# Ninety-two more products behind the last transposes of a fused convolution and two feed-forward layers

## The chip, the cores and the metric

The kernel runs on one core of a Trainium2 chip. The metric is the device time of one execution in microseconds. The kernel before took 1194.71 and 1194.87 us in two runs, with a median of 1194.79.

## The reference

Two batches of 4096 tokens with 192 numbers each go through a short causal convolution (7 taps, weights by softmax, one set for each of 8 groups of 24 columns) and then through two feed-forward layers with 2048 hidden columns. Everything is fp32.

```python
w = np.exp(weight - weight.max(-1)); w = w / (w.sum(-1) + 1e-09)
out = np.einsum('hk,bskhg->bshg', w, x_unf)      # 7 taps along the sequence
h = x @ w_in;  g = np.maximum(0.01 * h, h);  x = g @ w_out
h = x @ w_in;  g = np.where(h >= 1, h, np.where(h <= -1, 0.0, (h + 1) ** 2 / 4));  out = g @ w_out
```

## The kernel before, in words

The 8192 tokens are cut into 16 blocks of T = 512. A block is held transposed: the 192 columns lie on partitions, 128 of them and 64 of them (DB), and the 512 tokens along the line. An fp32 value is split into a high and a low part of type fp32r, so that one exact product becomes several products of fp32r: x has the parts 0 and 1 for the first 128 columns and 2 and 3 for the other 64, stored twice on 128 partitions; the weights are wi_h, wi_l, wi_b and wo_h, wo_l, wo_b, each a resident tile of 16 chunks of 128 columns (NF = 16, 2048 numbers in a line).

The unit of work is one block, one layer and one chunk of 128 hidden columns. Its `up` (L584) does five products into a bank of PSUM, the other engines apply the activation and split the result into gh and gl, and its `down` (L593) does five products into two accumulator banks. There are 2 x 16 x 16 = 512 units, ten products each, 5120 in all; every product loads its own stationary tile of 128 x 128 and streams 512 columns.

Every step is given to a planner with an engine, a cost and a due time; it simulates the engines, and the steps are then issued in the order of their planned starts (`plan.order()`, the loop at the end of the kernel). Each engine works through its own list in this order.

At the start there are products of zeros in bf16 (L328), transposes of the input for the first three blocks (L478; 128 columns, or 64 for the second part), and some taps of the convolution as products in plain fp32 with a diagonal matrix (L529, with `rhs=t()[:, 1, 2 * k:2 * k + T]`, and L534); each product of plain fp32 stands as two records in the trace. In the first and the second layer together the units' banks are 0 to 3, the accumulators of the first layer 4 and 5, of the second 6 and 7.

The last block ends in `finish_last`. ACT copies one accumulator (L691), DVE the other (L692); the tensor engine turns them back with four products by an identity (L697, into bank 1) and four transposes (L706, into bank 0); DVE and ACT copy these into two output tiles (L714, L723), and each of the two tiles goes to memory with one transfer (L732), one issued by SP's queue and one by ACT's. The four transposes are the last entries of the tensor engine's list. At the end of the program SP's queue waits for the transfers, and then all engines meet (L803, the launch).

Of the kernel before, what the change touches and what calls it, by code (L numbers as in the profile page):

```python
# [145 lines left out]
def kernel(  # L146
# [16 lines left out]
    nc = tc.nc  # L163
# [6 lines left out]
    T = 512  # L170
# [34 lines left out]
    banks = [pp.tile([128, T], F32, name=f"bank{i}") for i in range(8)]  # L205
# [22 lines left out]
    wi_h = [cp.tile([128, NF, 128], F32R, name=f"wi_h{m}") for m in range(2)]  # L228
    wi_l = [cp.tile([128, NF, 128], F32R, name=f"wi_l{m}") for m in range(2)]
    wi_b = [cp.tile([128, NF, 128], F32R, name=f"wi_b{m}") for m in range(2)]  # L230
    wo_h = [cp.tile([128, NF, 128], F32R, name=f"wo_h{m}") for m in range(2)]
# [89 lines left out]
    def add_warm():  # L321
        nc.gpsimd.memset(zero, 0.0)
        out_ = bank(1, -10)
        for i in range(WARM):
            cold = i < COLD
            plan.add(
                pe, 430 if cold else 220,
                lambda: nc.tensor.matmul(  # L328
                    out=out_(), lhsT=zero, rhs=zero.unsqueeze(1).broadcast_to((128, T // 128, 128)),
                    start=True, stop=True,  # L330
                ),
                writes=[out_], due=-1e9 if cold else 1e9,
            )
# [53 lines left out]
    def add_diagonals():  # L387
        def fold():
            for e in range(2):
                nc.gpsimd.tensor_copy(same[DB * e:DB * (e + 1)], ident[DB * e:DB * (e + 1), DB * e:DB * (e + 1)])  # L390

        plan.add(pool, 500, lambda: make_identity(nc, ident), writes=["ident"])
        plan.add(pool, 260, fold, reads=["ident"], writes=["same"])
        for k in range(KP, K):
            plan.add(
                dve, 220,
                lambda k=k: nc.vector.tensor_scalar(flat(NP + k - KP), ident, taps[:, 0, k:k + 1], None, ALU.mult),
                reads=["ident", "taps"], writes=[("diagonal a", k)], uses=[spare],
            )
        for k in range(NP):  # L400
            plan.add(
                dve, 220,
                lambda k=k: nc.vector.tensor_scalar(
                    flat(k).rearrange("p (e d) -> p e d", e=2), same.unsqueeze(1).broadcast_to((128, 2, DB)),
                    pair[:, k:k + 1], None, ALU.mult,
                ),
                reads=["same", "pair"], writes=[("diagonal", k)], uses=[spare],
            )
# [327 lines left out]
            )  # L736


    units = []
    for i in range(NF + OFF[-1]):  # L740
        for j in range(N0):
# [2 lines left out]
    one = [(0, j, f) for j in range(N0, NB) for f in range(NF)]  # L744
    two = [(1, j, f) for j in range(NB) for f in range(NF)]
    while two:
        units += one[:1] + two[:1]
        one, two = one[1:], two[1:]
# [12 lines left out]
    with tc.manual_schedule():  # L761
        add_warm()
        add_taps()
        add_diagonals()
        seen = set()
        for t, (m, j, f) in enumerate(units):
            if m == 0 and f == 0:
                add_conv(t - AHEAD, j)
            for o in range(2):
                if (m, o, f // 2) not in seen:  # L770
                    seen.add((m, o, f // 2))
                    add_weights(t, m, o, f // 2)
            add_unit(t, (m, j, f))
        for tag, count in COUNT.items():
            plan.rotate(tag, count)
        for n in plan.order():
            plan.steps[n]["fn"]()


# [28 lines left out]
```

## Time and profile before

| what | before |
|---|---|
| median of two runs | 1194.79 us (1194.71 and 1194.87) |
| profiled execution, first to last instruction (span) | 1192.7 us |
| around the span | not recorded for the profiled execution; the two runs are 2.0 and 2.2 us longer than its span |
| tensor engine busy | 1186.8 us, 5210 products |
| weight loads | 972.7 us, 5210 |
| VectorE (DVE), ScalarE (ACT), GpSimd (POOL) busy | 782.7, 734.3, 438.2 us |
| mean granted clock of the tensor engine | 0.999 of 2.4 GHz |

PE stands for the tensor engine's products, PEld for its weight loads, which run beside the products. The records of consecutive products overlap, since a product takes longer from its start to its end than the next one has to wait; so the cost of a product in a stream is the distance from start to start. An instruction's line in the trace is the line of the kernel shown above. "x8" after a row means that eight instructions stand in it, and the time is from the first start to the last end.

### The profile page before, as it was taken

The numbers are of one execution on the slowest core, as the hardware profiler recorded it, in microseconds if no ns is written. First come the engines' busy times: TensorE is split into PE (matmuls) and PEld (weight loads), VectorE is DVE, ScalarE is ACT, GpSimd is POOL, SyncE is SP. The second block draws the span as 40 slices with busy tenths as digits, with TensorE's granted clock in tenths as the row PEclk, the third lists the DMA queues.
The fourth block names the chain that finished last, engine by engine and source line by source line (L and its number), as shares of the span: only waits on it lengthen the run. The fifth ranks groups of instructions, "written<-read, shape, count | busy, mean of one in ns | idle before, by whom it ended". The sixth has DMA issues, their size and how long they took to land.

```text
span 1192.7 us, 15464 instructions
## 1 busy us (share of the span) xinstructions
PE 1186.8 (100%) x5210; PEld 972.7 (82%) x5210; DVE 782.7 (66%) x1209; ACT 734.3 (62%) x1296; POOL 438.2 (37%) x407
## 2 busy tenths in 40 slices
PE   9999999999999999999999999999999999999998
PEld 5788888888888888888888888888888888888887
DVE  7899897748567494764847658485674545447664
ACT  6777866656565565655656566565655656556654
POOL 4566374323223232232323233232233222335554
PEclk9999999999999999999999999999999999999999
DMA  4443111101001010010101001010000000000000
GB/s 132 117 104 99 43 43 18 23 1 23 10 9 23 1 23 9 15 18 1 32 1 23 10 10 23 1 23 1 1 14 1 14 1 3 12 1 14 14 14 14
DMA packets 114000, 27.90 MB, mean 23 GB/s; under 512 B 103680, under 2 KB 111872, under 8 KB 113920
## 3 DMA queue, kind: packets, MB, share of 16 engines
q1 hardware_dynamic: 113504, 26.69, 10.3%
q8 instruction: 40, 0.66, 0.2%
q14 instruction: 40, 0.33, 0.1%
q10 hardware_dynamic: 416, 0.23, 0.1%
HBM read 20.61 MB, written 6.29 MB: 23 GB/s over the span
## 4 chain that ended last, share of the span: by engine, by line
PE 99%; DMA 0%; SPq 0%; DVE 0%; issue 0%; ACT 0%; ACTq 0%
PE bank L584 49%; PE bank L593 49%; PE bank L529 1%; DMA wraw<-in_x_dram 0%; PE bank L534 0%; PE bank L328 0%; PE bank L478 0%; SPq L257 0%; PE bank L697 0%; SPq L255 0%; DVE s L714 0%; SPq L469 0%; DVE s L723 0%; ACT s L723 0%; ACTq L723 0%
## 5 line engine op out<-in xcount | busy, mean ns | idle before, releaser
L632 POOL TENSOR_TENSOR gl<-g,gh 128x512 fp32r<-128x512 f32 x256 | 343.2, 1343 | 677.6 <-ACT gh L630 674.7
L619 DVE TENSOR_SCALAR s<-bank 128x512 f32<-128x512 f32 x256 | 176.3, 689 | 303.4 <-PE bank L584 302.2
L584 PE MATMUL bank<-x,wi_h 128*128 128x512 f32 x1024 | 317.5, 391 | 0.0
L584 PE MATMUL bank<-x,wi_b 128*128 128x512 f32 x1024 | 316.9, 391 | 0.0
L623 ACT ACTIVATE s<-s,half 128x512 f32<-128x512 f32 x256 | 184.8, 722 | 192.7 <-DVE s L619 191.4
L630 ACT CAST gh<-g 128x512 fp32r<-128x512 f32 x256 | 158.6, 620 | 180.8 <-DVE g L627 178.1
L584 PEld LDWEIGHTS bank<-x,wi_h 128*128 128x128 f32 x1024 | 191.9, 188 | 42.2 <-issue 1.7
L584 PEld LDWEIGHTS bank<-x,wi_b 128*128 128x128 f32 x1024 | 192.2, 188 | 41.4 <-issue 1.4
L627 DVE TENSOR_TENSOR g<-bank,s 128x512 f32<-128x512 f32 x256 | 175.5, 686 | 67.8 <-ACT s L623 67.7
L593 PE MATMUL bank<-gh,wo_b 128*128 128x512 f32 x512 | 199.3, 389 | 0.0
L593 PE MATMUL bank<-gh,wo_h 128*128 128x512 f32 x512 | 199.3, 389 | 0.0
L593 PE MATMUL bank<-gl,wo_h 128*128 128x512 f32 x512 | 199.2, 389 | 0.0
L584 PE MATMUL bank<-x,wi_l 128*128 128x512 f32 x512 | 199.2, 389 | 0.0
L593 PE MATMUL bank<-gl,wo_b 128*128 128x512 f32 x512 | 199.2, 389 | 0.0
L593 PE MATMUL bank<-gh,wo_l 128*128 128x512 f32 x512 | 199.2, 389 | 0.0
L608 ACT ACTIVATE gh<-bank 128x512 fp32r<-128x512 f32 x256 | 152.8, 597 | 46.8 <-PE bank L593 25.3
L612 DVE TENSOR_TENSOR gl<-bank,gh 128x512 fp32r<-128x512 f32 x256 | 174.2, 680 | 9.8 <-ACT bank L608 9.2
L608 ACT ACTIVATE bank<-bank 128x512 f32<-128x512 f32 x256 | 151.8, 593 | 0.0
L523 DVE SCALAR_TENSOR_TENSOR xy<-xT,taps,xy 128x512 f32<-128x512 f32 x159 | 136.0, 878 | 0.2
L593 PEld LDWEIGHTS bank<-gl,wo_h 128*128 128x128 f32 x512 | 96.1, 188 | 20.0
L593 PEld LDWEIGHTS bank<-gh,wo_b 128*128 128x128 f32 x512 | 96.1, 188 | 20.0
L593 PEld LDWEIGHTS bank<-gh,wo_h 128*128 128x128 f32 x512 | 96.1, 188 | 20.0
(93 smaller groups left out, 741.5 us busy)
## 6 DMA issues: line engine op xcount, KB each, us to landing
xy<-in_x_dram SPq DMA_DIRECT2D x104, 64.0 KB, 2.4
wraw<-in_moe_w_out_dram SPq DMA_DIRECT2D x16, 384.0 KB, 3.0
out_dram<-o SPq DMA_DIRECT2D x90, 64.0 KB, 1.9
wraw<-in_moe_w_in_dram SPq DMA_DIRECT2D x16, 256.0 KB, 2.7
wraw<-in_moe_w_in_dram SPq DMA_DIRECT2D x32, 64.0 KB, 2.6
wraw<-in_x_dram SPq DMA_DIRECT2D x3, 384.0 KB, 5.3
out_dram<-s SPq DMA_DIRECT2D x1, 192.0 KB, 2.0
out_dram<-s ACTq DMA_DIRECT2D x1, 192.0 KB, 2.0
```

Of the source, the lines that this page charges most:

```text
L523: nc.vector.scalar_tensor_tensor(out=ys[i](), in0=t()[:, i, k:k + T], scalar=taps[:, i, k:k + 1], in1=ys[i](), op0=ALU.mult, op1=ALU.add,)
L529: nc.tensor.matmul(out=ys[1](), lhsT=flat(k), rhs=t()[:, 1, 2 * k:2 * k + T], start=(k == 0), stop=(k == NP - 1))
L584: nc.tensor.matmul(out=h(), lhsT=w, rhs=v[:, k], start=(part == 0 and i == 0), stop=(part == 1 and i == 1))
L593: nc.tensor.matmul(out=p[part](), lhsT=w, rhs=v(), start=(first and i == 0), stop=(last and i == len(todo) - 1))
L608: lambda dst=dst: nc.scalar.activation(out=dst(), in_=h(), func=ACTF.Prelu, alpha=0.01),
L612: dve, 680, lambda: nc.vector.tensor_tensor(out=b(), in0=h(), in1=a(), op=ALU.subtract),
L619: dve, 680, lambda: nc.vector.tensor_scalar(s(), h(), 1.0, -1.0, ALU.min, ALU.max),
L623: act, 720, lambda: nc.scalar.activation(out=s(), in_=s(), func=ACTF.Square, scale=0.5, bias=half),
L627: dve, 680, lambda: nc.vector.tensor_tensor(out=g(), in0=h(), in1=s(), op=ALU.max),
L630: plan.add(act, 620, lambda: nc.scalar.copy(a(), g()), reads=[g], writes=[a])
L632: pool, 1390, lambda: nc.gpsimd.tensor_tensor(out=b(), in0=g(), in1=a(), op=ALU.subtract),
```

## The change

A function `add_more` is called after the planner's last step, so its products stand behind everything else on the tensor engine's list. Each multiplies a stationary tile from the first layer's wo_h (at column q) with a moving operand from the first layer's wi_h (from column o), both resident since the start, into a bank of PSUM that nobody reads afterwards. Twelve groups of four differ in o and q alone, then come four with 64 columns in the stationary tile, four that stream 256 columns, four that take every second number, four on the lower 64 rows of the array into one bank, twelve that alternate between the lower and the upper 64 rows, three groups of lower, upper and two full ones, and four full ones. None waits for another engine, and the output is not touched.

```diff
+    def add_more():
+        flat_m, flat_w = wi_h[0].rearrange("p f c -> p (f c)"), wo_h[0].rearrange("p f c -> p (f c)")
+        n = [0]
+        def one(o, q, rows=slice(0, 128), cols=128, length=T, step=1, at=None):
+            bank_ = banks[2 + n[0] % 2 if at is None else at]
+            n[0] += 1
+            nc.tensor.matmul(
+                out=bank_[0:cols, 0:length], lhsT=flat_w[rows, q:q + cols],
+                rhs=flat_m[rows, o:o + step * length:step], start=True, stop=True,
+            )
+        def four(**how):
+            for _ in range(4):
+                one(**how)
+        for o, q in ((0, 0), (384, 0), (128, 0), (256, 0), (0, 64), (0, 4), (0, 2), (4, 0), (2, 0), (64, 64), (64, 0), (4, 4)):
+            four(o=o, q=q)
+        four(o=0, q=0, cols=64)
+        four(o=0, q=0, length=256)
+        four(o=0, q=0, step=2)
+        low, high = slice(0, 64), slice(64, 128)
+        four(o=0, q=0, rows=low, at=2)
+        for _ in range(6):
+            one(o=0, q=0, rows=low, at=2)
+            one(o=0, q=0, rows=high, at=3)
+        for _ in range(3):
+            one(o=0, q=0, rows=low, at=2)
+            one(o=0, q=0, rows=high, at=3)
+            one(o=0, q=0, at=4)
+            one(o=0, q=0, at=5)
+        four(o=0, q=0)
...
         for n in plan.order():
             plan.steps[n]["fn"]()
+        add_more()
```

At the end of the tensor engine's list (bank_64 is bank 0, bank_66 bank 2, and so on; wi_h_82 and wo_h_88 are the first layer's tiles; the shape is the output's), the piece of the difference where the added rows begin, without the 90 that follow:

```order
 L697 MATMUL bank_65<-same,yz 128x64 x4
 L706 MATMUL bank_64<-ident,xy 128x128 x4
-L803 UNCONDITIONAL_BRANCH
+L747 MATMUL bank_66<-wi_h_82,wo_h_88 128x512
+L747 MATMUL bank_67<-wi_h_82,wo_h_88 128x512
```

The eight rows of the output stage stay where they are, and the branch that ended the list now stands behind the added products.

In the list after the change, on the tensor engine, the last full products of the placements and then the narrow and the short ones:

```order
L747 MATMUL bank3_67<-wi_h0_82,wo_h0_88 128x512
L747 MATMUL bank2_66<-wi_h0_82,wo_h0_88 64x512
L747 MATMUL bank3_67<-wi_h0_82,wo_h0_88 64x512
L747 MATMUL bank2_66<-wi_h0_82,wo_h0_88 64x512
L747 MATMUL bank3_67<-wi_h0_82,wo_h0_88 64x512
L747 MATMUL bank2_66<-wi_h0_82,wo_h0_88 128x256
L747 MATMUL bank3_67<-wi_h0_82,wo_h0_88 128x256
```

These stood nowhere before; the two banks alternate, and no other engine's work stands between them.

Also on the tensor engine after the change, the first mixed group of four: the lower half of the rows into bank 2, the upper into bank 3, then two full products into banks 4 and 5:

```order
L747 MATMUL bank2_66<-wi_h0_82,wo_h0_88 128x512
L747 MATMUL bank3_67<-wi_h0_82,wo_h0_88 128x512
L747 MATMUL bank4_68<-wi_h0_82,wo_h0_88 128x512
L747 MATMUL bank5_69<-wi_h0_82,wo_h0_88 128x512
L747 MATMUL bank2_66<-wi_h0_82,wo_h0_88 128x512
```

The rows do not tell half a product from a full one, since the output has the same shape; the bank does, here. The lists of the other four engines have the same rows as before.

## Rows read from the trace of the kernel before

**Rows 1.** The page's first part: busy us (share of the span) x instructions.

```profile
PE 1186.8 (100%) x5210; PEld 972.7 (82%) x5210; DVE 782.7 (66%) x1209; ACT 734.3 (62%) x1296; POOL 438.2 (37%) x407
```

**Rows 2.** The granted clock in 40 equal slices, in tenths (9 is 90% or more).

```profile
PEclk9999999999999999999999999999999999999999
```

**Rows 3.** The chain of work that ended last, by engine and by line.

```profile
PE 99%; DMA 0%; SPq 0%; DVE 0%; issue 0%; ACT 0%; ACTq 0%
PE bank L584 49%; PE bank L593 49%; PE bank L529 1%; DMA wraw<-in_x_dram 0%; PE bank L534 0%; PE bank L328 0%; PE bank L478 0%; SPq L257 0%; PE bank L697 0%; SPq L255 0%; DVE s L714 0%; SPq L469 0%; DVE s L723 0%; ACT s L723 0%; ACTq L723 0%
```

**Rows 4.** Timeline, steady stretch of the tensor engine: start us, us, engine, line, operation.

```profile
1162.03 0.39 PE L593 MATMUL bank<-gl,wo_h 128*128 128x512 f32 x1
1162.26 0.62 PE L584 MATMUL bank<-x,wi_h 128*128 128x512 f32 x2
...
1173.59 0.62 PE L584 MATMUL bank<-x,wi_h 128*128 128x512 f32 x2
```

**Rows 5.** Timeline, the last six microseconds, all engines.

```profile
1186.98 0.39 PE L593 MATMUL bank<-gl,wo_h 128*128 128x512 f32 x1
1187.36 0.97 PEld L697 LDWEIGHTS bank<-same,yz 128*128 128x128 f32 x8 [0.41 <-ACT yz L691]
1187.36 1.10 PE L697 MATMUL bank<-same,yz 128*128 128x64 f32 x8
...
1188.30 0.61 PE L706 MATMUL bank<-ident,xy 128*128 128x128 f32 x4
...
1189.40 0.39 SPq L732 DMA_DIRECT2D out_dram<-s  x1
1189.46 0.37 ACT L723 COPY s<-bank 128x256 f32<-128x256 f32 x1 [2.15 <-DVE s L723]
1189.86 0.40 ACTq L732 DMA_DIRECT2D out_dram<-s  x1
```

**Rows 6.** The last transfers' issues (KB each, us to landing), and SP's queue: what it waited for.

```profile
out_dram<-s SPq DMA_DIRECT2D x1, 192.0 KB, 2.0
out_dram<-s ACTq DMA_DIRECT2D x1, 192.0 KB, 2.0
...
SPq L803 <- DMA out_dram<-s: 1.8, 2, 1.4
SPq L803 <- PEq L803: 0.6, 2, 0.4
```

**Rows 7.** Timeline, other forms of product early in the program.

```profile
13.09 2.73 PE L529 MATMUL bank<-xT,x 128*128 128x512 f32 x6
...
17.26 0.39 PE L328 MATMUL bank<-zero 128*128 128x512 bf16 x1
...
18.10 1.47 PE L328 MATMUL bank<-zero 128*128 128x512 bf16 x6
19.41 0.59 PE L529 MATMUL bank<-xT,x 128*128 128x512 f32 x1
```

**Rows 8.** Timeline, transposes with 64 and with 128 columns between full products.

```profile
25.16 0.60 PE L478 MATMUL bank<-ident,wraw 128*64 128x128 f32 x4
...
25.51 0.70 PE L584 MATMUL bank<-x,wi_h 128*128 128x512 f32 x2
...
26.05 0.39 PE L584 MATMUL bank<-x,wi_l 128*128 128x512 f32 x1
...
26.75 0.60 PE L478 MATMUL bank<-ident,wraw 128*128 128x128 f32 x4
...
27.10 0.48 PE L593 MATMUL bank<-gh,wo_b 128*128 128x512 f32 x1
...
27.41 0.40 PE L593 MATMUL bank<-gl,wo_b 128*128 128x512 f32 x1
```

**Rows 9.** Lines 697 and 706: duration of one, ns, least/median/most.

```profile
L697 PE MATMUL bank<-same,yz x8: 275/275/324, 1187.4 to 1188.2; 128*128 128x64 f32 x8
...
L706 PE MATMUL bank<-ident,xy x4: 272/272/280, 1188.3 to 1188.6; 128*128 128x128 f32 x4
```

**Rows 10.** Stretches: us, busy of five engines, granted clock, DMA share, GB/s.

```profile
1187.00:1189.00 2.00, 1.91 (x14) 1.31 (x12) 1.19 (x4) 0.31 (x1) 0.00 (x0) 1.00 0.00 0
1189.00:1191.00 2.00, 0.00 (x0) 0.00 (x0) 0.37 (x1) 0.37 (x1) 0.00 (x0) 1.00 0.36 121
1191.00:1191.50 0.50, 0.00 (x0) 0.00 (x0) 0.00 (x0) 0.00 (x0) 0.00 (x0) 0.60 0.90 303
1191.50:1192.70 1.20, 0.00 (x0) 0.00 (x0) 0.00 (x0) 0.00 (x0) 0.00 (x0) 0.50 0.00 0
```

## The prediction

> **What bounds the kernel now.** I read the page's busy times first, then the chain of work that ended last, then the steady stretch, the last six microseconds and the first thirty. The tensor engine is busy for 1186.8 of 1192.7 us [rows 1], its granted clock is at its upper level all along [rows 2], and the chain that ended last is 99% tensor engine, in halves L584 and L593 [rows 3]. So the kernel is one long list of products, and whatever is put on that list without cover shows in the time. What one product costs is read from the distance between starts, not from the record's own length, because the records overlap. In a steady stretch the same place of the pattern starts at 1162.26 and at 1173.59 us, five rounds of ten products apart: 11.33 / 50 = 0.2266 us each; a record there reads 0.39, so a product ends 0.39 - 0.23 = 0.16 us after the next one could start [rows 4].
>
> The last microseconds decide what the change can hide under. The four transposes of L706 start at 1188.30 and last 0.61 in all, the last record 0.27, so their starts are (0.61 - 0.27) / 3 = 0.11 apart, the last at 1188.64, and the next product on the list could start at 1188.75 [rows 5]. After that the tensor engine has nothing to do in the kernel before; the output goes on alone: copies, then two transfers issued at 1189.40 and 1189.86 that land 2.0 us after their issue, the last at about 1191.9 [rows 5, 6]. From there to the end of the span are 0.8 us, in which SP's queue waits for the tensor engine's queue and the others (0.6 us over two waits) [rows 6]. The exposed end behind the tensor engine's list is thus 1192.7 - 1188.75 = 3.95 us.
>
> **The change part by part.** Nothing is removed and nothing is moved. 92 products are put behind the transposes, on the tensor engine alone; no one waits for them except the end of the program. They write banks 2 to 5, which nobody uses any more, and the copies of the output read banks 0 and 1, so the output's 3.1 us run beside them untouched. If that cover were missing, with the output first, the 3.1 us would come on top.
>
> What the list costs, by the row nearest to each kind:
> - 48 products in twelve placements, 128 x 128 on 512 columns: the form of the steady stretch, 48 x 0.2266 = 10.88 us. In no row of before does such a product start anywhere but on a multiple of 128 numbers. The nearest rows are the taps: six records of L529 (three products, offsets of 2, 4 and 6 numbers into their operand) keep (2.73 - 0.59) / 5 = 0.43 apart, twice 0.216 and no more [rows 7]. They are products of plain fp32, two records each at half the pace, so they would hide a slower read up to a point. I take no cost; from below a product can go down to the bf16 pace, (1.47 - 0.39) / 5 = 0.216 [rows 7]; from above up to 0.43.
> - 4 with a stationary tile of 64 columns: 4 x 0.2266 = 0.91. Four transposes with 64 columns between full products take (26.05 - 25.16) - 2 x 0.2266 = 0.44 us, and four with 128 columns (27.41 - 26.75) - 0.2266 = 0.43 [rows 8]: narrowing costs nothing and saves nothing.
> - 4 on 256 columns: between the pace of loads, which the eight short records of L697 show as (1.10 - 0.28) / 7 = 0.118 each [rows 5, 9], and 0.2266. Half of 0.2266 is 0.113, so I take 0.118: 0.47.
> - 4 that read every second number: no row; 0.2266 to 0.43, I take the lower: 0.91.
> - 4 on the lower half of the rows, one after the other into one bank: 0.2266 each, 0.91.
> - 12 that alternate between the lower and the upper half, and 3 x 2 more such pairs inside mixed groups of four: no row shows half the array at work. Above, they follow one another at 0.2266; below, a second one starts as soon as its weights are in, 0.118. The two halves share no rows of the array, no partitions of their operands and no bank, so I take the lower: 9 pairs x 0.236 = 2.12; one after the other it would be 4.08.
> - 6 full ones in the mixed groups and 4 at the end: 10 x 0.2266 = 2.27.
>
> Sum: 10.88 + 0.91 + 0.47 + 0.91 + 0.91 + 2.12 + 2.27 = 18.47 us. Between the shapes the array's division changes eight times (to 64 columns and back, to half the rows, then out, in, out, in, out). The columns' change costs less than 0.01 us by the fours above [rows 8]; for the rows' change I take nothing, and 0.16 at most, the part of a record that sticks out past the next start [rows 4].
>
> One rule of the Trainium skill speaks against that: TensorEngine Tiling (Array Packing), section Tiling Modes, says that a change of the tiling mode, not of the tile alone, drains the engine. By it the eight changes would cost 8 x 0.16 = 1.3 us more; the transposes of 64 columns, 0.44 us for four against 0.43, do not bear it out for columns, and no row of before shows it for rows.
>
> The end: the list starts at 1188.75, its last record ends 18.47 + 0.16 us later, at 1207.38. What follows is the end of the program, for which I take the same 0.8 us that stand behind the last landing now: 1208.2. The old span was 1192.7, so the change costs 15.5 us: 18.47 + 0.16 less the 3.15 us by which the output outlives the transposes. That is the span of one profiled execution; the two runs shown lie 2.0 and 2.2 us above it, and I expect that distance to stay. 1194.8 + 15.5 = 1210.3 us, 1.3% more. About 2% (23.9 us, to 1218.7) is what a measurement of this kernel can tell from no change, so the forecast is: no change by that measure, though every microsecond of it will be there.
>
> **The rivals.**
> 1. *The halves do not run together.* For it: all products of before stand in strict order and no record shows two at work. Against it: separate rows, partitions and banks. It costs 4.08 - 2.12 = 1.96 us: 1212.3.
> TensorE: Matmul & The Clock Gate, Part 3, in the Trainium skill says that products on different row groups run at the same time, which is this rival's opposite; no row here shows it.
> 2. *Every change of shape drains the engine.* A record's overhang of 0.16 us [rows 4] is paid eight times: 1.3 us, 1211.6. Against it stand the transposes [rows 8].
> It is the drain rule named above; by it, 1211.6.
> 3. *Placement costs a second pass.* Products whose operand does not start on a multiple of 128 numbers, or steps by two, take the 0.43 of L529's records [rows 7]. That is eight of the twelve placements and the strided four, 36 x (0.43 - 0.2266) = 7.3 us: 1217.6. For it: no row of before has such a start in this form. Against it: L529 and its offsets [rows 7].
> 4. *The clock falls, and the kernel is slower by over 2%.* The granted clock drops to 0.60 and then to 0.50, the 1.2 GHz level, between 1191.0 and 1191.5 us, about two microseconds after the last transpose [rows 10]. If the added list, of which some works on half the array, let it drop, each product at half the clock would cost twice as much: 18.5 us more over the whole list, 1228.8. The forecast leaves 23.9 - 15.5 = 8.4 us to the bound, so it decides once the lower level holds for 45% of the list. Against it: the clock stayed up through the 0.4 us that L697 waits [rows 5, 10], and the added list has no waits at all.
> 5. *The products are not there, or lie beside something.* Their sums are not read. Dropped, they would leave 1194.8. Against it: all 92 stand in the built program's list, on the engine that ends last.
>
> **How the numbers follow.** Forecast 0.52, rival 1 0.25, rival 2 0.11, rival 3 0.07, rival 4 0.04, rival 5 0.01. The low end: every full product at 0.216 (79 slots x 0.0106 = 0.8 us less), and an end of program of half its 0.8 us, 0.4 less, with 1.6 us over for what no row shows, such as loads of equal weights that cost less: 1207.5. The high end: rivals 1 and 2 together, 15.5 + 1.96 + 1.3 = 18.8, that is 1213.6, and ten products at the doubled pace, 2.0 more: 1215.6, taken as 1215.5. Left out are most of rival 3, and rivals 4 and 5, about 0.1. Slower by over 2% needs rival 4, or rival 3 together with 1: 0.05. Faster by over 2% has no mechanism: 0.01.
>
> **What would show it.** Right: L747 as a group of 92 that starts at 1188.7 to 1188.8 us and whose first 48 starts lie 0.227 apart, whatever the placement; four starts 0.12 apart at 256 columns; upper-half products that start 0.12 after the lower; the granted clock at 1.00 to the end; the output's transfers issued at 1189.4 and 1189.9 as now; the span 1208 us. Wrong, step by step: starts 0.43 apart at one placement (rival 3), 0.227 between the halves (rival 1), a gap of 0.16 us at each change of shape (rival 2), a granted clock of 0.50 before 1207 us (rival 4). Outside 1207.5 to 1215.5 the sum itself is wrong.

## The result and the profile after

The changed kernel takes 1212.18 us (1212.10 and 1212.26) against 1194.79 us before: a ratio of 1.0147 with a 95% interval of 1.0118 to 1.0176. That is 17.4 us more, inside the range given and 1.9 us over the number given; by the bound of 2% it is no change. The span of the profiled execution grew from 1192.7 to 1210.4 us.

The page of the kernel after, busy time and the chain that ended last; the second row answers to [rows 1]:

```profile
span 1210.4 us, 15648 instructions
...
PE 1207.6 (100%) x5302; PEld 987.3 (82%) x5302; DVE 782.3 (65%) x1209; ACT 734.3 (61%) x1296; POOL 438.2 (36%) x407
...
PE 99%; DMA 0%; SPq 0%; POOL 0%; issue 0%; POOLq 0%
PE bank L584 48%; PE bank L593 48%; PE bank L747 2%; PE bank L529 1%; DMA wraw<-in_x_dram 0%; PE bank L534 0%; PE bank L478 0%; PE bank L328 0%; POOL x L426 0%; SPq L257 0%; PE bank L697 0%; SPq L255 0%; PE bank L706 0%; SPq L469 0%; POOLq L487 0%
```

All 92 products are there (5302 against 5210), the other engines do what they did, and L747 has become 2% of the chain that ended last, where [rows 3] ended with the output's copies.

The timeline of the end after, all engines, which answers to [rows 5]:

```profile
1187.21 1.10 PE L697 MATMUL bank<-same,yz 128*128 128x64 f32 x8
...
1188.15 0.61 PE L706 MATMUL bank<-ident,xy 128*128 128x128 f32 x4
...
1188.52 0.71 PE L747 MATMUL bank<-wi_h,wo_h 128*128 128x512 f32 x2
...
1189.25 0.39 SPq L732 DMA_DIRECT2D out_dram<-s  x1
1189.31 0.37 ACT L723 COPY s<-bank 128x256 f32<-128x256 f32 x1 [2.15 <-DVE s L723]
1189.72 0.41 ACTq L732 DMA_DIRECT2D out_dram<-s  x1
```

Everything up to the list runs 0.15 us earlier than in the profiled execution of before, and the output's two transfers keep their places in it: they lie beside the list. The waits of SP's queue in the last stretch (in total, times, longest) show who is late now, against [rows 6] (L839 is the line that was L803):

```profile
SPq L839 <- PE bank L747: 19.7, 1, 19.7
SPq L839 <- PEq L839: 0.6, 2, 0.4
```

The end of the program waited 1.8 us for the output; now it waits 19.7 us for the tensor engine.

The added list by kind, in stretches cut at the starts of its groups. The list is counted from 1188.60: its first record starts at 1188.52, but the second only at 1188.83, one product of 0.227 after 1188.60. Each row has us, busy time of PE, PEld, DVE, ACT, POOL, granted clock, DMA share and GB/s; a product that overlaps a border counts twice. The rows are twelve placements in two halves, 64 columns, 256 columns, step 2, the block on half the rows, the mixed groups, the last four.

```profile
1188.60:1194.05 5.45, 5.45 (x26) 4.51 (x25) 0.62 (x3) 0.37 (x1) 0.00 (x0) 1.00 0.21 72
1194.05:1199.61 5.56, 5.56 (x26) 4.46 (x24) 0.00 (x0) 0.00 (x0) 0.00 (x0) 1.00 0.00 0
1199.61:1200.53 0.92, 0.92 (x6) 0.59 (x4) 0.00 (x0) 0.00 (x0) 0.00 (x0) 1.00 0.00 0
1200.53:1201.00 0.47, 0.47 (x5) 0.47 (x4) 0.00 (x0) 0.00 (x0) 0.00 (x0) 1.00 0.00 0
1201.00:1202.90 1.90, 1.90 (x7) 0.61 (x5) 0.00 (x0) 0.00 (x0) 0.00 (x0) 1.00 0.00 0
1202.90:1205.64 2.74, 2.74 (x20) 1.97 (x19) 0.00 (x0) 0.00 (x0) 0.00 (x0) 1.00 0.00 0
1205.64:1208.41 2.77, 2.77 (x12) 1.45 (x11) 0.00 (x0) 0.00 (x0) 0.00 (x0) 1.00 0.00 0
1208.41:1209.35 0.94, 0.94 (x5) 0.56 (x3) 0.00 (x0) 0.00 (x0) 0.00 (x0) 1.00 0.00 0
```

The list took 1209.35 - 1188.60 = 20.75 us where 18.47 were foreseen. Placements, 64 columns, 256 columns and the last four came out as foreseen within 0.13 us each. Two kinds did not. The four with step 2 took 0.45 us each, twice a plain product: 1.8 us, 0.88 too many (the row's last 0.11 is the change to half the rows). The half-row block and the mixed groups took 5.62 us from 1202.79 to 1208.41, where 4.39 were foreseen: 1.23 too many. The granted clock is at its upper level throughout.

My theory after this: reading every second number costs a second pass, and each of the six changes of the array's division between all rows and half of them costs 0.2 us. The rivals: placements or the halves themselves cost the time; narrowing the columns pays as well; the clock has a part in it. There was also a smaller thing to explain, that from the twenty-fifth added product on, full ones start 0.232 apart and no longer 0.227 (5.56 us for 24 against 5.45).

### The profile page after: what moved, and what is told of

It reads as the page before. It is cut to its first block, busy times and chain, and to the rows that moved or that the text cites. A ratio compares the mean times of both kernels' runs of the same rounds, so it can differ in the third digit from the quotient of the medians.

```text
span 1210.4 us, 15648 instructions
## 1 busy us (share of the span) xinstructions
PE 1207.6 (100%) x5302; PEld 987.3 (82%) x5302; DVE 782.3 (65%) x1209; ACT 734.3 (61%) x1296; POOL 438.2 (36%) x407
## 4 chain that ended last, share of the span: by engine, by line
PE 99%; DMA 0%; SPq 0%; POOL 0%; issue 0%; POOLq 0%
PE bank L584 48%; PE bank L593 48%; PE bank L747 2%; PE bank L529 1%; DMA wraw<-in_x_dram 0%; PE bank L534 0%; PE bank L478 0%; PE bank L328 0%; POOL x L426 0%; SPq L257 0%; PE bank L697 0%; SPq L255 0%; PE bank L706 0%; SPq L469 0%; POOLq L487 0%
```

## The experiments

Each kernel has another list in place of the 92, and the same program ahead of it. In the differences, against the changed kernel, `...` stands for rows that are not shown, and rows without a sign are in both. The kernel before, run beside them, took 1194.40, 1194.63 and 1194.43 us (median of each set).

**e1: one placement.**

```diff
...
-            four(o=o, q=q)
...
+        for _ in range(92):
+            one(o=0, q=0)
```

> The added list is 92 full products of one and the same placement (both operands from column 0), alternating between two banks. My theory: the pace of a full product does not hang on where its operands start, and the 0.232 us between starts seen after the 24th added product comes from something else, so it appears here too: the first 24 starts 0.227 apart, the rest about 0.232, the list about 21.2 us and the span about 1210.8. Rival (placement costs 5 ns a product): 0.2267 from the first start to the last, 20.9 us, span about 1210.4.

Measured: span 1210.6 us (1212.34 us).

```profile
1188.65:1190.73 2.08, 2.08 (x11) 1.69 (x10) 0.62 (x3) 0.37 (x1) 0.00 (x0) 1.00 0.25 86
1190.73:1209.55 18.82, 18.82 (x84) 15.39 (x82) 0.00 (x0) 0.00 (x0) 0.00 (x0) 1.00 0.03 11
```

After nine products at 0.231 the other 83 go at 18.82 / 83 = 0.2267 to the end. My expectation was wrong: the place in the list is not what slows the later products.

**e2: the placements turned round.**

```diff
-        for o, q in ((0, 0), (384, 0), (128, 0), (256, 0), (0, 64), (0, 4), (0, 2), (4, 0), (2, 0), (64, 64), (64, 0), (4, 4)):
+        for o, q in ((0, 0), (384, 0), (128, 0), (256, 0), (0, 64), (0, 4), (0, 2), (4, 0), (2, 0), (64, 64), (64, 0), (4, 4))[::-1]:
             four(o=o, q=q)
...
+        for o, q in ((2, 0), (0, 0), (0, 2), (0, 0), (2, 2), (0, 0)):
+            for _ in range(8):
+                one(o=o, q=q)
```

> The twelve placements in the opposite order (first both operands 4 columns in, last both from column 0), then groups of eight that start 2 columns in, in the moving operand, in the stationary one or in both, with groups of eight from column 0 between them: 96 full products. If placement sets the pace, the first 32 products here go at 0.232 and the groups from column 0 return to 0.227. If it is the place in the list, the first 24 go at 0.227 whatever their operands, and the groups from column 0 at 0.232 like their neighbours. Span about 1211.5 either way.

Measured: span 1211.7 us (1213.43 us). The stretches are the first 32 products, the next 16 (whose operands start on multiples of 128 numbers), and the first of the groups of eight: (2, 0) and (0, 0).

```profile
1188.55:1195.95 7.40, 7.40 (x34) 6.01 (x33) 0.61 (x3) 0.37 (x1) 0.00 (x0) 1.00 0.16 53
1195.95:1199.58 3.63, 3.63 (x17) 3.00 (x16) 0.00 (x0) 0.00 (x0) 0.00 (x0) 1.00 0.00 0
1199.58:1201.46 1.88, 1.88 (x10) 1.51 (x9) 0.00 (x0) 0.00 (x0) 0.00 (x0) 1.00 0.00 0
1201.46:1203.31 1.85, 1.85 (x10) 1.50 (x9) 0.00 (x0) 0.00 (x0) 0.00 (x0) 1.00 0.00 0
```

The first 32 go at 0.231, the 16 aligned ones at 0.227, and then (2, 0) at 0.235 and (0, 0) at 0.231 like its neighbours. Neither expectation holds alone: with e1 it reads as a pace that some placements disturb and that plain products get back after a while. How long that takes differs: nine products in e1, at most one or two here (the 16 aligned ones go at 0.227 in the mean), while the first plain group of eight behind (2, 0) stays at 0.231. What the disturbance is, and what ends it, stays open; it is at most 0.008 us a product, and 0.1 us in the changed kernel.

**e3: steps and lengths.**

```diff
...
+        for step in (1, 2, 1, 3, 1, 4, 1):
+            for _ in range(8):
+                one(o=0, q=0, step=step)
+        for length in (64, 128, 256, 384, 512):
+            for _ in range(8):
+                one(o=0, q=0, length=length, step=2)
```

> Groups of eight with steps of 1, 2, 1, 3, 1, 4, 1 through the moving operand, then groups of eight with step 2 and 64, 128, 256, 384 and 512 columns. My theory: every step over 1 costs the same second pass, 0.45 us for 512 columns, so steps of 2, 3 and 4 cost alike (3.6 us for eight) and the cost grows with the columns, 0.88 ns each, down to the pace of loads (0.12). Rival (the cost goes with the distance, as lines of memory touched): step 3 about 0.56 to 0.68 and step 4 about 0.9. By the first the 96 products take 8 x (4 x 0.227 + 3 x 0.45) = 18 us and the short ones 8 x (0.12 + 0.12 + 0.23 + 0.34 + 0.45) = 10 us.

Measured: span 1217.9 us (1219.64 us). Eight products each with step 2, 3 and 4, then step 2 with 256, 384 and 512 columns:

```profile
1190.45:1194.05 3.60, 3.60 (x10) 1.64 (x8) 0.00 (x0) 0.00 (x0) 0.00 (x0) 1.00 0.26 85
...
1195.90:1199.47 3.57, 3.57 (x9) 1.64 (x8) 0.00 (x0) 0.00 (x0) 0.00 (x0) 1.00 0.00 0
...
1201.31:1204.98 3.67, 3.67 (x10) 1.64 (x9) 0.00 (x0) 0.00 (x0) 0.00 (x0) 1.00 0.00 0
...
1208.63:1210.47 1.84, 1.84 (x10) 1.67 (x9) 0.00 (x0) 0.00 (x0) 0.00 (x0) 1.00 0.00 0
1210.47:1213.22 2.75, 2.75 (x9) 1.67 (x8) 0.00 (x0) 0.00 (x0) 0.00 (x0) 1.00 0.00 0
1213.22:1216.83 3.61, 3.61 (x9) 1.45 (x7) 0.00 (x0) 0.00 (x0) 0.00 (x0) 1.00 0.00 0
```

3.60, 3.57 and 3.67: a step of 3 or 4 costs what a step of 2 costs, and the cost grows with the columns, 0.23, 0.34, 0.45 us each. The rival by distance falls. That the engine goes over the operand twice is a picture of mine; what the runs show is the price.

**e4: many changes of shape.**

```diff
...
+        for _ in range(12):
+            one(o=0, q=0, at=2)
+            one(o=0, q=0, rows=low, at=3)
         for _ in range(6):
...
+            for i in range(4):
+                one(o=0, q=0, at=2 + i % 2)
+            for i in range(4):
+                one(o=0, q=0, rows=low, at=4 + i % 2)
         four(o=0, q=0)
+        for _ in range(12):
+            one(o=0, q=0, at=2)
+            one(o=0, q=0, cols=64, at=3)
```

> Twelve times one full product and one on the lower half of the rows; then six times four full and four on the lower half; four full; twelve times one full product and one with 64 stationary columns. My theory: each change between all rows and half the rows costs 0.2 us, narrowing the columns nothing: the first part is 24 x 0.227 + 24 x 0.2 = 10.2 us, the second 48 x 0.227 + 12 x 0.2 = 13.3 us, the third 24 x 0.227 = 5.4 us (0.23 between starts). Rival (the mode is a tile size, so columns pay as well): the third takes 10.2 us like the first. Rival (the lost time of the mixed groups came from the pairs, not from the change): 5.4, 10.9 and 5.4 us.

Measured: span 1234.7 us (1236.43 us), 15 us more than the theory's list would have given. The stretches: alternation of full and half up to the fall of the clock; its rest; the fours; then, from start to start, 20 products that alternate between 128 and 64 columns.

```profile
1188.60:1194.45 5.85, 5.85 (x16) 2.53 (x14) 0.68 (x3) 0.37 (x1) 0.00 (x0) 1.00 0.20 67
1194.50:1201.79 7.29, 7.29 (x12) 2.86 (x11) 0.00 (x0) 0.00 (x0) 0.00 (x0) 0.50 0.00 0
1201.79:1225.83 24.04, 24.04 (x50) 13.88 (x49) 0.00 (x0) 0.00 (x0) 0.00 (x0) 0.50 0.00 0
1228.82:1233.42 4.60, 4.60 (x22) 3.22 (x20) 0.00 (x0) 0.00 (x0) 0.00 (x0) 1.00 0.00 0
```

Up to 1194.5 us the starts are 0.43 apart, 0.227 and 0.2 for the change, as expected. Then the granted clock falls to 0.50, the 1.2 GHz level, after 5.9 us in which the engine changed its division at every product, and it comes back at 1228.6, 2.8 us after the last half-row product gave way to full rows. In between a product with its change takes 0.73 us, and the 48 in fours 24.04 us where 13.3 were expected. The alternation of columns, at the upper level, takes 4.60 / 20 = 0.230, the slower of the two paces of e1 and e2: narrowing pays nothing that could be told from it. So rival 4 of the prediction is real, though it was not in the changed kernel.

The timeline shows what else a change does. In the steady stretch of before a weight load starts 0.22 us ahead of its product, beside the product ahead of it (the first two rows); at a change (e4, the last two) load and product start together:

```profile
1184.02 0.19 PEld L593 LDWEIGHTS bank<-gh,wo_h 128*128 128x128 f32 x1
1184.24 0.39 PE L593 MATMUL bank<-gh,wo_h 128*128 128x512 f32 x1
...
1190.25 0.19 PEld L747 LDWEIGHTS bank<-wi_h,wo_h 128*128 128x128 f32 x1 [0.24 <-issue]
1190.25 0.50 PE L747 MATMUL bank<-wi_h,wo_h 128*128 128x512 f32 x1
```

The load's 0.19 us, hidden in a stream, come close to the price of a change. That they are the whole price, and why the load does not start ahead, is not shown.

**e5: the halves in order and out of it.**

```diff
...
-        for _ in range(6):
+        for _ in range(24):
             one(o=0, q=0, rows=low, at=2)
             one(o=0, q=0, rows=high, at=3)
...
+        for _ in range(22):
+            one(o=0, q=0, rows=low, at=4)
+        for _ in range(22):
+            one(o=0, q=0, rows=high, at=5)
```

> 24 times one product on the lower and one on the upper half of the rows, then 22 on the lower half alone into one bank, then 22 on the upper half alone into another. My theory: the two halves run together whatever the order on the list, so that queued upper products start beside lower ones ahead of them: a pair costs 0.233 us, the 24 pairs 5.6 us, and the 44 that follow well under 44 x 0.227 = 10.0 us, 5.1 us if all overlap; list 10.9 to 13 us, span about 1200.5 to 1203. Rival (products start in list order): pairs 5.6 us, then 10.0 us, list 15.6 us, span about 1205.3.

Measured: span 1204.7 us (1206.38 us). Pairs; the lower ones alone; a stretch of eight starts; then, from the timeline, the records that overlap 1190.05 us.

```profile
1188.80:1194.38 5.58, 5.58 (x49) 4.59 (x49) 0.52 (x2) 0.37 (x1) 0.00 (x0) 1.00 0.21 70
1194.38:1198.46 4.08, 4.08 (x20) 3.31 (x18) 0.00 (x0) 0.00 (x0) 0.00 (x0) 1.00 0.00 0
1198.46:1199.27 0.81, 0.81 (x9) 0.76 (x8) 0.00 (x0) 0.00 (x0) 0.00 (x0) 1.00 0.00 0
...
1189.83 0.62 PE L747 MATMUL bank<-wi_h,wo_h 64*128 64x512 f32 x4
1190.05 0.19 PEld L747 LDWEIGHTS bank<-wi_h,wo_h 64*128 64x128 f32 x2
```

48 half products in 5.58 us: a pair costs 0.23 us, what one full product costs. Four records, two pairs, take 0.62 us, 0.23 and one record of 0.39, and two loads take 0.19 like one: the two of a pair load and start together. The queue of lower ones behind them goes at 4.08 / 18 = 0.227 with nothing beside it, until four of them are left; then eight products start in 0.81 us. Since lower ones alone start 0.227 apart (e7), the additional starts must be upper ones that run ahead of the last lower ones. So a product can start beside an earlier one, but only a few places ahead on the list (how the list is looked through is not shown): mine was half right, and the span is near the rival's. The order on the list has to be close to pairs.

**e6: both undone.**

```diff
...
-        four(o=0, q=0, step=2)
...
+        four(o=0, q=0)
+        for _ in range(6):
+            one(o=0, q=0, at=4)
         four(o=0, q=0, rows=low, at=2)
-        for _ in range(6):
+        for _ in range(9):
             one(o=0, q=0, rows=low, at=2)
             one(o=0, q=0, rows=high, at=3)
...
         four(o=0, q=0)
```

> The changed kernel's 92 products with two things undone: the four of step 2 read with step 1, and all products on half the rows stand in one block (two changes between all rows and half of them where there were six). My theory: 0.88 us for the step and 4 x 0.2 us for the changes go away, the list takes 19.1 us instead of 20.75 and the span falls by 1.7 us, from 1210.4 to 1208.7; time about 1210.5. Rival (the lost time lies in the placements and in the halves themselves): the span stays at 1210.4 within 0.3.

Measured: span 1208.8 us, median 1210.65 us (1210.55 to 1210.86), ratio to before 1.0135 (1.0118 to 1.0152). The block on half the rows, with 22 products, and the last four with the way back to all rows:

```profile
1203.54:1206.73 3.19, 3.19 (x23) 2.33 (x23) 0.00 (x0) 0.00 (x0) 0.00 (x0) 1.00 0.00 0
1206.73:1207.77 1.04, 1.04 (x5) 0.67 (x4) 0.00 (x0) 0.00 (x0) 0.00 (x0) 1.00 0.00 0
```

1.6 us of the span are gone with the same number of products, where 1.7 were expected. The rival falls: it is neither the placements nor the halves.

**e7: half the rows alone.**

```diff
...
+        low = slice(0, 64)
+        for i in range(92):
+            one(o=0, q=0, rows=low, at=2 + i % 2)
```

> 92 products on the lower half of the rows alone, alternating between two banks. My theory: it was the changes between all rows and half of them, each with its pause, that let the clock fall in the kernel with many changes; half the rows alone keep the engine busy and the granted clock at 1.00: 92 x 0.227 = 20.9 us, span about 1210.6. Rival (work on half the rows counts for too little by itself): the granted clock falls to 0.50 some 6 us into the list, and the rest goes at 0.43: list about 35 us, span about 1225.

Measured: span 1210.9 us (1212.61 us).

```profile
1188.60:1209.60 21.00, 21.00 (x94) 16.96 (x93) 0.77 (x3) 0.37 (x1) 0.00 (x0) 1.00 0.06 19
```

21.0 us at a granted clock of 1.00: half the rows cost what all cost, and in this list the clock did not fall under them alone.

**e8: the mixed group 23 times.**

```diff
...
+        for _ in range(23):
             one(o=0, q=0, rows=low, at=2)
             one(o=0, q=0, rows=high, at=3)
             one(o=0, q=0, at=4)
             one(o=0, q=0, at=5)
-        four(o=0, q=0)
```

> The changed kernel's mixed group (lower half, upper half, two full) 23 times in place of three: 46 changes. At the pace of the three groups measured, 1.10 us each, the list takes 25.2 us and the span is about 1214.9, if the granted clock stays at 1.00. If the changes let it fall as in the kernel that alternates full and half (half of the time lost there, here 38%), it falls to 0.50 about 6 us into the list, and the list takes 35 to 42 us.

Measured: span 1214.8 us (1216.50 us). The stretch holds 21 groups:

```profile
1189.91:1212.73 22.82, 22.82 (x87) 10.15 (x86) 0.00 (x0) 0.00 (x0) 0.00 (x0) 1.00 0.05 17
```

1.087 us a group. Three starts at 0.2267 would be 0.68, so the two changes cost 0.41, 0.2 each, without wear over 46 of them. The clock stayed up here, and fell in e4 after 14 products. What tells the two apart was not tried further and stays open.

**e9: how the operand is read.**

```diff
...
+        def own(lhsT, rhs):
+            for _ in range(8):
+                bank_ = banks[2 + n[0] % 2]
+                n[0] += 1
+                nc.tensor.matmul(out=bank_, lhsT=lhsT, rhs=rhs, start=True, stop=True)
+
+        w, v = flat_w[:, 0:128], flat_m[:, 0:T]
+        own(w, v)
+        own(flat_w[:, 0:256:2], v)
+        own(flat_w[:, 0:512:4], v)
+        own(w, v)
+        for t in (2, 4, 8, 1):
+            own(w, flat_m[:, 0:2 * T].rearrange("p (m s t) -> p m s t", s=2, t=t)[:, :, 0, :])
+        own(w, v)
+        own(zero, zero.unsqueeze(1).broadcast_to((128, 4, 128)))
+        own(zero, zero[:, 0:128:2].unsqueeze(1).broadcast_to((128, 8, 64)))
+        own(zero, zero[:, 0:128:4].unsqueeze(1).broadcast_to((128, 16, 32)))
```

> Groups of eight products of 512 columns that differ in how the operands are read: plain; stationary tile with step 2; with step 4; plain; moving operand as every other pair of numbers; every other four; every other eight; every other one; plain; then products of zeros in bf16, plain, with every second and with every fourth number. My theory: the engine takes two neighbouring fp32 numbers (8 bytes) per read, so single numbers cost a second pass and pairs none: 0.227 between starts for pairs, fours and eights, 0.45 for singles; a stepped stationary tile takes twice as long to load (0.21 instead of 0.12), still inside the 0.227 of its product; bf16 at 0.216 plain, and slower with steps (0.43) if it is the neighbours that count. Rival (a line of 16 bytes must be used twice, or the whole of it counts): pairs and singles with step 2 use the same half of each line, so pairs cost 0.45 like singles, and fours 0.227; bf16 with a step of 2 uses four numbers of a line and stays at 0.216.

Measured: span 1217.2 us (1218.93 us). Stationary tile with step 2 and with step 4; every other pair, four, eight and single number of the moving operand; bf16 plain, with step 2, with step 4; eight products each.

```profile
1190.56:1192.43 1.87, 1.87 (x9) 1.58 (x8) 0.00 (x0) 0.00 (x0) 0.00 (x0) 1.00 0.49 165
1192.43:1194.31 1.88, 1.88 (x10) 1.84 (x9) 0.00 (x0) 0.00 (x0) 0.00 (x0) 1.00 0.00 0
...
1196.15:1199.75 3.60, 3.60 (x9) 1.64 (x8) 0.00 (x0) 0.00 (x0) 0.00 (x0) 1.00 0.00 0
1199.75:1201.63 1.88, 1.88 (x9) 1.52 (x8) 0.00 (x0) 0.00 (x0) 0.00 (x0) 1.00 0.00 0
1201.63:1203.50 1.87, 1.87 (x9) 1.51 (x8) 0.00 (x0) 0.00 (x0) 0.00 (x0) 1.00 0.00 0
1203.50:1207.13 3.63, 3.63 (x10) 1.65 (x8) 0.00 (x0) 0.00 (x0) 0.00 (x0) 1.00 0.00 0
...
1209.00:1210.74 1.74, 1.74 (x10) 0.80 (x9) 0.00 (x0) 0.00 (x0) 0.00 (x0) 1.00 0.00 0
1210.74:1212.55 1.81, 1.81 (x10) 0.77 (x9) 0.00 (x0) 0.00 (x0) 0.00 (x0) 1.00 0.00 0
1212.55:1216.14 3.59, 3.59 (x9) 0.79 (x7) 0.00 (x0) 0.00 (x0) 0.00 (x0) 1.00 0.00 0
```

Pairs cost as much as singles (3.60 and 3.63), fours and eights as little as a plain read (1.88 and 1.87). So my theory of pairs falls and the rival's pattern holds: full pace where four fp32 numbers stand together, half where two or one do. In bf16 a step of 2 costs 0.226 against 0.217, and only a step of 4 costs 0.45. In both types four numbers out of 16 bytes keep the pace (or nearly, in bf16) and two do not; three were not tried. A stepped stationary tile stays hidden inside its product.

**e10: the step alone undone.**

```diff
-        four(o=0, q=0, step=2)
+        four(o=0, q=0)
```

> The changed kernel with the four stepped products read with step 1, all else as it is (the six changes between all rows and half of them remain). My theory: 4 x (0.45 - 0.227) = 0.9 us less, span 1209.5, so that the rest of the 1.7 us that the kernel with both things undone gained, 0.8 us, is the four changes more. Rival (the changes were cheap and the step took nearly all): span 1208.7 to 1208.9.

Measured: span 1209.6 us (1211.37 us). The four products and the change behind them, 1.90 us in the changed kernel:

```profile
1201.15:1202.17 1.02, 1.02 (x6) 0.57 (x4) 0.00 (x0) 0.00 (x0) 0.00 (x0) 1.00 0.00 0
```

The step is worth 0.88 us in this stretch and 0.8 us of the span, and the further 0.8 us between this kernel and e6 (1208.8) is what four changes less are worth. Spans of one kernel differ by some tenths (before: 1192.6 to 1193.1 us), so the size of each term rests on the stretches. Both terms stand by themselves, and together they make up what e6 gained.

## Why the prediction was right, and where its number was off

The frame held. The kernel's end hangs on the tensor engine's list, the products stood behind the transposes with no cover, the output's 3.1 us lay beside them, and nothing before the list changed places. Counted from 1188.60, the list started 0.15 us earlier than reckoned, with everything ahead of it (its first record, at 1188.52, lies outside the 1188.7 to 1188.8 named as a sign), and the end of the program took 0.9 us behind the last record where 0.8 were taken.

Term by term:
- 48 placements: 10.88 foreseen, 11.01 measured. That placement costs nothing was right within 0.13 us; rival 3 is wrong in this part.
- 64 columns 0.91 and 0.92; 256 columns 0.47 and 0.47, at the pace of loads taken from L697; the last four 0.91 and 0.94.
- Step 2: 0.91 foreseen, 1.79 measured. The step that failed is "0.2266 to 0.43, I take the lower": I had no row and chose the end that cost nothing. The upper end, 0.43, was nearly the price (0.45), and for this part rival 3 was right. The Trainium skill has a rule for it, in SBUF — State Buffer, Specifications: a line of 16 bytes needs at least two uses for full bandwidth. Read as enough, this would make a step of 2 in fp32 free; e3 and e9 measured 0.45 against 0.227, two numbers of four did not keep the pace, and four did.
- The halves: running together, 9 pairs at 0.236, was right (0.23 in e5) and rival 1 is wrong. The way to the number was not: it put the second of a pair one load, 0.118, behind the first, where the two start together (e5) and the next pair follows at a full product's pace. That twice 0.118 lies so near is luck.
- Changes of division: "for the rows' change I take nothing" failed. Six changes cost 1.23 us, 0.2 each, confirmed by e8, and by e10 against e6. This is rival 2 in its place: it was priced 0.16 for each of eight; measured are 0.2 for six and nothing for the two of the columns. Its picture, the part of a record that sticks out, is not what the trace shows: there a load of 0.19 us no longer runs ahead (e4). I had carried the transposes' evidence, which shows a change of columns, over to a change of rows. The rule of the Trainium skill that the prediction weighed (TensorEngine Tiling (Array Packing), Tiling Modes: a change of mode drains the engine) fits the price of the rows' changes in the changed kernel, e6 and e8; for columns no such price is seen (e4: 0.230).

The two failed terms are 0.88 + 1.23 = 2.1 us of the 2.28 by which the list was longer; with the earlier start, the longer end and the runs that lie 1.7 to 1.8 us above the span and not 2.1, they leave the 1.9 us by which the number was low. The 2.0 and 2.2 us had set two runs against the span of another execution: where a run of the kernel before is recorded with its own span, the distance is 1.7 to 1.8 us too (1194.40 against 1192.7 beside e1). The range held because its high end had 1.3 us for rival 2 and 2.0 us for ten products at the doubled pace.

No version that beats the kernel before came out of this: all that was added lies on the path that ends last, and even with both dear terms undone the 92 products cost 16.0 us (e6, 1210.65 against 1194.63).

## What to carry to other kernels

Where a kernel ends on one engine's list, price additions by start-to-start distances of that very form, and where no row shows a form, weigh its costly end by what the operation changes (the direction of the change, the way of reading) and not by what looks alike. Products on half the rows pay only as neighbouring pairs and in one block, since each way in or out costs 0.2 us here and in e4 many of them in a row were followed by a fall of the clock. Lay out a moving operand of fp32 so that at least four numbers stand together; a step inside that doubled the time of the product (in bf16 a step of 2 cost only 4%).

## What I had not expected of the hardware

- The clock fell to 1.2 GHz under a list that waits for no other engine: it fell after 5.9 us of alternation between full and half-row products (e4, one run), and it stayed there for 34 us, through groups of four and four. 92 half-row products (e7) and 46 changes at 1.09 us for four (e8) left it up.
- A product on the upper half of the rows can start before earlier ones on the lower half that are still queued, about four places ahead (e5).
- Plain products of one form have more than one pace, 0.2267 and 0.231 to 0.235, and after a disturbance return to the first after one or two products (e2) or after nine (e1); why is open.
- At a change between all rows and half of them, the weight load does not run ahead beside the product before it but starts with its own product (e4).
